# Two attention and feed-forward layer pairs on one core: fixed queue order at the start, two tiles transposed by DMA, and rstd of one chunk on ScalarE

## The chip, the cores and the metric

The kernel runs on one core of a Trainium2 chip. The metric is device time in microseconds for one whole execution, lower is better. The engines are TensorE (PE in the profile; its weight loads are PEld), VectorE (DVE), ScalarE (ACT), GpSimd (POOL) and SyncE (SP), which here only issues DMAs. Each engine works through its own queue in order; engines wait for one another by semaphores.

## The reference

Two times over, a linear attention block and a feed-forward block are added to x (2048 tokens, D = 512):

```python
x = x + A(layernorm(x));  x = x + B(layernorm(x))      # twice, with the same weights

def A(x):                         # 32 heads of 16
    q, k, v = split(x @ wqkv)
    phi = lambda t: where(t > 0, t + 1, exp(t)) + 1e-6
    kv  = einsum("bhsd,bhse->bhde", phi(k), v);  z = sum_s phi(k)
    o   = (phi(q) @ kv) / (phi(q) . z + 1e-6)
    return o @ wo                 # 512 x 512

def B(x):
    return relu(x @ w1) @ w2      # 512 -> 1376 -> 512
```

Inputs, weights and the output are bfloat16; matrix products accumulate in float32 and x is kept in float32 between the layers.

## The kernel before, in words

The tokens are cut in 16 tiles of 128, which make 4 chunks of 4 tiles. A tile has its tokens on the partitions. All of x, all weights and all intermediate results stay in on-chip memory; only x, the weights and the result are moved from and to HBM. There are four layers, 0 to 3: attention, feed-forward, attention, feed-forward.

**Attention (layers 0 and 2).** Each normalized tile xn[i] is transposed to Tb[i]. kproj i multiplies it by the k columns of wqkv (4 matmuls of 128x512, contracted over the four parts c of D). The phi function follows: ACT writes t + 1 (line 532, "lin") and exp(t) (line 534, "exp"), DVE takes the minimum with 1 (line 536, "em") and the maximum of both (line 542, "phi"). qproj t_j does the same for a chunk t and a quarter j of the q columns; it needs all four tiles of the chunk. The G groups (g_r, g_a) multiply the xn of a chunk by phi(k) and accumulate over all chunks; a column of ones, written over the last column of xn by POOL (line 582, "onec"), gives the sums z there. From G and the v weights the kernel makes kv, masks it by heads and multiplies it by wo (Mf). wv needs its last row taken off first (line 577). The denominators (den) are turned into reciprocals rdc by Ln and Exp on ACT (lines 653, 655), spread over the partitions by DMA (line 665, "spread") and multiplied into phi(q) by DVE (line 671, "pqs"). The fin matmuls multiply that by Mf, and DVE adds the result to x (line 560, "resid") with the row sums s1 as a by-product; ACT squares the new x (line 566) for the row sums of squares s2.

**Feed-forward (layers 1 and 3).** w1 times Tb of a chunk gives eleven strips h; relu is applied by ACT or DVE (lines 743, 744). The last strip, 96 wide (hr), is made transposed and turned by a DMA transpose (line 724). ffo i multiplies the strips by w2 (11 matmuls), and DVE adds x (line 560, or 557 in the last layer). In the last layer tile 15 is made in two halves of 256 columns (b_out_halves, line 748), each with its own add (line 762) and store (line 765).

**Normalization.** In the first layer the statistics come from bn_stats and bn_aggr on DVE (lines 446, 447). Tiles 0, 1 and 2 are taken one at a time (line 793): veps on DVE (811), rstd by a power on POOL (801), norm on DVE (803), then a transpose on PE against the identity (line 514) and a copy out of PSUM by ACT or DVE (518, 519, "trev"). Tile 3 has its sums from ACT (814, 816) and its variance from POOL (818 to 822, "nm2_3", "var_3", "veps_3"). Chunk 1 (tiles 4 to 7) is taken in pairs, with rstd by Ln and Exp on ACT (454, 456), norm on DVE (480) and transposes on PE. Chunks 2 and 3 are taken whole and transposed by DMA from SP (line 497, tr2_0, tr2_1, tr3_0). Between the layers, ln_next makes mean, variance, rstd and nbias of a chunk in seven small POOL instructions (462 to 474, the sixth a power of 1.0 to 1.3 us), then norms on DVE, ACT and, for the last tile of the chunk, POOL (484 to 489), and transposes by DMA. Chunk 0 of a feed-forward layer is "urgent": its transposes go in two halves.

**What sets the order.** The program builds a graph of operations with their data dependencies, and `_list_schedule` (line 136) plays it through with fixed estimates of duration. On each engine it takes the operation that can start first, and among those that could start at once the one with the lowest priority number; that number is the place in the program plus an entry of HINTS, if there is one. Operations with alternatives (add_flex) go to the engine that would finish them first. The result is a fixed queue for each engine, so the order on the chip doesn't react to real durations. Eleven matmuls on zeros warm PE up first (line 423). The loads are issued by SP in the order of the program: x of tile 0, x of tiles 1 to 3, wk, x of chunk 1, wq, x of chunks 2 and 3, wv, the last row of wv, wo, w1, w2 in two parts. The first DMA transpose also waits for wk and wq.

Of the kernel before, what the change touches and what calls it, by code (L numbers as in the profile page):

```python
# [7 lines left out]
ALU = alu_op_type.AluOpType  # L8
# [39 lines left out]
HINTS = {"0.bnag4": 3, "0.fin8_0": -99, "0.g0_1_3": 10, "0.g1_1_1": 30, "0.g1_2_1": -496, "0.g1_2_2": -77, "0.k0_em": -57,  # L48
         "0.k4_em": -180, "0.k5_em": -110, "0.pqs3_3": 37, "0.q0_0_em": 80, "0.q0_2_em": -70, "0.q0_2_phi": 30, "0.q0_3_em": 33,
         "0.q3_2_lin": 177, "0.q3_3_lin": 30, "0.resid8": -373, "0.rstd6": 20, "0.spread1_3": -17, "0.trev1": 10, "2.fin13_0":  # L50
         200, "2.fin9_0": 200, "2.g0_0_0": 80, "2.norm0": -160, "2.q3_3_lin": 3, "2.qproj3_1": 10, "2.qproj3_2": -80,
         "2.spread0_0": 3, "2.spread0_3": -230, "2.spread1_0": 30, "2.spread1_2": 57, "2.var1": 610, "3.ffo10": 84, "3.ffo15_h1":
         200, "3.ffo2": 200, "3.h1_9_0": 230, "3.h3_3_0": 83}
# [209 lines left out]
def build_kernel(nc, A_x, A_wqkv, A_wo, B_w1, B_w2, out, n_layers_pairs=2, K_STT=0, Q_STT=0, A_PE_CHUNKS=0, windows=None,  # L263
# [20 lines left out]
    with es:  # L284
# [109 lines left out]
        dma(lambda e: e.dma_start(wqkv[:, :, D:2 * D], wq_v[:, :, D:2 * D]), [], [("wk",)], 2300.0, "ld_wk")  # L394
# [15 lines left out]
        ALL_LOADS = [("wk",), ("wq",)]  # L410
# [48 lines left out]
        def ln_chunk(t):  # L459
# [8 lines left out]
            g.add(POOL, lambda e: e.tensor_tensor(var[:, sl], s2[:, sl], nm2[:, sl], ALU.add),  # L468
                  [("s2", i) for i in tl] + [("nm2", t)], [("var", i) for i in tl], C_POOL_SMALL, name="var%d" % t)
            g.add(POOL, lambda e: e.tensor_scalar(veps[:, sl], var[:, sl], INV_D, EPS, ALU.mult, ALU.max),  # L470
                  [("var", i) for i in tl], [("veps", t)], C_POOL_SMALL + 50.0, name="veps%d" % t)
            g.add(POOL, lambda e: e.tensor_tensor(rstd[:, sl], veps[:, sl], nhalf[:, 0:4], ALU.pow),  # L472
                  [("veps", t), ("nhalf",)], [("rstd", i) for i in tl], C_POOL_POW, name="rstd%d" % t)
            g.add(POOL, lambda e: e.tensor_tensor(nbias[:, sl], mean[:, sl], rstd[:, sl], ALU.mult),  # L474
                  [("mean", i) for i in tl] + [("rstd", i) for i in tl], [("nbias", t)], C_POOL_SMALL, name="nbias%d" % t)

        def ln_norm(i, first, urgent=False):
# [7 lines left out]
            if i % 4 == 3:  # L485
                g.add(POOL, ts[1], [("xres", i), ("rstd", i), ("mean", i)], [("xn", i)], ts[2], name="norm%d" % i)
                return
# [4 lines left out]
        def transpose_chunk(t, extra_reads=(), parts=1):  # L492
            n = 4 // parts
            for k in range(parts):
# [7 lines left out]
        def transpose_pe(i):  # L502
# [19 lines left out]
            if i == 0:  # L522
                part(0, 2, ("T0a",), "0a")
                part(2, 2, ("T", 0), "0b")
                return
# [43 lines left out]
        def a_k(i):  # L569
            b = alloc_bank()  # L570
            mm_group(lambda: [(psv[:, b, :], Tb[:, i, c, :], wqkv[:, c, D:2 * D], c == 0, c == 3, False) for c in range(4)],
                     [("T", i), ("wk",)] + ([("T0a",)] if i == 0 else []), [("ps", b)], 4 * C_MM512, "kproj%d" % i)
            phi_evac(b, pk_tile(i), ("big", pk_unit(i)), "k%d" % i, stt=(i % 4) < K_STT)
# [64 lines left out]
        def a_q(t, js=(0, 1, 2, 3)):  # L638
            for j in js:
# [3 lines left out]
                         [("T", i) for i in range(4 * t, 4 * t + 4)] + ([("T0a",)] if t == 0 else []) + [("wq",)], [("ps", b)], 4 * C_MM512, "qproj%d_%d" % (t, j))  # L643
# [104 lines left out]
        def b_out_halves(i):  # L748
            t, il = i // 4, i % 4
            for hf in range(2):  # L750
                b = alloc_bank()

                def mk(b=b, hf=hf):
                    mms = []
                    for c in range(NFC):
                        K = 128 if c < NFC - 1 else FLAST
                        u = h_unit(c, t)
                        mms.append((psv[:, b, 0:256], big[0:K, u * 512 + 128 * il:u * 512 + 128 * il + 128],
                                    w2[0:K, c, 256 * hf:256 * hf + 256], c == 0, c == NFC - 1, False))
                    return mms  # L760
                mm_group(mk, [("big", h_unit(c, t)) for c in range(NFC)] + W2KEYS, [("ps", b)], NFC * 110.0, "ffo%d_h%d" % (i, hf))
                g.add(DVE, lambda e, b=b, hf=hf: e.tensor_tensor(xin[:, i, 256 * hf:256 * hf + 256], psv[:, b, 0:256],  # L762
                                                                 xres[:, i, 256 * hf:256 * hf + 256], ALU.add),
                      [("ps", b), ("xres", i)], [("xinh", i, hf)], 360.0, name="resid_out%d_%d" % (i, hf))
                dma(lambda e, hf=hf: e.dma_start(tok_view(out, t, il, il + 1)[:, 0, 256 * hf:256 * hf + 256], xin[:, i, 256 * hf:256 * hf + 256]),
                    [("xinh", i, hf), ("xin", i)] + [("T", k) for k in range(NT)], [("out", "h", i, hf)], 250.0, "sth%d_%d" % (i, hf))

        def b_out(i, last_layer):
            if last_layer and LAST_HALVES and i == NT - 1:
                b_out_halves(i)  # L770
# [36 lines left out]
        def ln_first(t):  # L807
# [24 lines left out]
            for i in range(4 * t, 4 * t + 4):  # L832
                ln_norm(i, True)
                if t < FIRST_PE_CHUNKS:
                    transpose_pe(i)
            if t >= FIRST_PE_CHUNKS:
                tr_dma(t, 2 if t == 2 else 1)
# [3 lines left out]
        def tr_dma(t, parts=1):  # L841
            extra = list(ALL_LOADS) if tr_state["first"] else []
            tr_state["first"] = False
            transpose_chunk(t, extra, parts)
# [241 lines left out]
```

## Time and profile before

| | us |
|---|---|
| median of three runs | 283.12 |
| the three runs | 283.12, 282.18, 283.13 |
| the profiled execution | 282.23 |
| its span, first to last instruction | 280.5 |
| PE busy (matmuls) | 275.2 |
| ACT busy | 173.1 |
| DVE busy | 141.4 |
| POOL busy | 45.3 |

The granted TensorE clock is 1.000 over the whole span. In the views that follow, times are in microseconds from the start of the span, an "L" with a number is a line of the kernel, `out<-in` names what an instruction writes and reads, and a bracket at the end of a row gives the idle time of the engine before it and what ended it. In the chain that ended last, each row is a start, a length, and the work that held up the end in that stretch. Matmuls overlap in the records: one of 512 columns has 0.38 us of its own, while a dense stream starts one each 0.216 us. So a row of n matmuls is longer than n times the spacing.

### The profile page before, as it was taken

Reading aid. Unit: us, or ns where it says so; the run is one execution under the profiler, and the core shown is the slowest. Engines: PE = TensorE matmul, PEld = TensorE weight load, DVE = VectorE, ACT = ScalarE, POOL = GpSimd, SP = SyncE. Lnnn points to the kernel's source line nnn. Section 1 sums busy time; section 2 is a strip of 40 time slices with the busy share of each in tenths; the row PEclk is TensorE's granted clock in tenths of the full one; section 3 lists DMA queues with packets and bytes.
Section 4 is the critical chain, followed back from the end, with each engine's and each line's share of the span. In section 5 each row is a group of like instructions: output and inputs, shape, how many; then the busy total and the mean of one; then the engine's idle time right before and its main releaser. Section 6 shows DMA issues by size and latency. Waiting matters only on the chain.

```text
span 280.5 us, 4209 instructions
## 1 busy us (share of the span) xinstructions
PE 275.2 (98%) x1574; PEld 140.7 (50%) x1574; DVE 141.4 (50%) x380; ACT 173.1 (62%) x364; POOL 45.3 (16%) x122
## 2 busy tenths in 40 slices
PE   7999999999999999999999999999999999999996
PEld 2455556545554544544444455664554544454444
DVE  5999973899300361443363666279955200210222
ACT  4998988777764582677373898765884566025000
POOL 6100000055400160400040400004236100000000
PEclk9999999999999999999999999999999999999999
DMA  7999300833810054060003030084313600341012
GB/s 231 339 384 147 72 2 11 201 89 76 159 30 0 2 95 76 0 96 0 0 7 70 0 74 0 4 196 106 75 34 63 130 1 2 94 113 20 0 75 75
DMA packets 44260, 22.09 MB, mean 79 GB/s; under 512 B 34416, under 2 KB 42704, under 8 KB 44240
## 3 DMA queue, kind: packets, MB, share of 16 engines
q1 hardware_dynamic: 44240, 21.83, 32.7%
q8 instruction: 12, 0.20, 0.3%
q14 instruction: 8, 0.07, 0.1%
HBM read 7.14 MB, written 2.10 MB: 33 GB/s over the span
## 4 chain that ended last, share of the span: by engine, by line
PE 94%; DVE 2%; DMA 1%; POOL 1%; ACT 0%; issue 0%; SPq 0%; DVEq 0%; POOLq 0%
PE ps L549 93%; DMA xin<-in_A_x_dram 1%; DVE xres L560 1%; DVE bst L446 0%; POOL rstd L472 0%; DVE xn L484 0%; PE ps L514 0%; DVE big L671 0%; ACT big L532 0%; ACT Tb L518 0%; DVE xin L762 0%; SPq L389 0%; POOL mean L462 0%; DVE xn L803 0%; POOL veps L470 0%
## 5 line engine op out<-in xcount | busy, mean ns | idle before, releaser
L549 PE MATMUL ps<-w,big 128*128 128x512 bf16 (+2 forms) x363 | 77.4, 373 | 0.0
L549 PE MATMUL ps<-Tb,w 128*128 128x512 bf16 (+1 forms) x352 | 70.9, 360 | 0.0
L743 ACT ACTIVATE big<-ps 128x512 bf16<-128x512 f32 x70 | 41.8, 597 | 24.6 <-PE ps L549 24.4
L549 PEld LDWEIGHTS ps<-w,big 128*128 128x128 bf16 (+1 forms) x363 | 35.4, 98 | 40.7 <-ACT big L743 0.3
L549 PEld LDWEIGHTS ps<-Tb,w 128*128 128x128 bf16 x352 | 33.9, 98 | 32.8
L566 ACT ACTIVATE sqscr<-xres 128x512 bf16<-128x512 f32 x48 | 29.9, 623 | 31.2 <-DVE xres L560 30.9
L532 ACT ACTIVATE big<-ps 128x512 bf16<-128x512 f32 x64 | 40.8, 641 | 7.1 <-PE ps L549 6.9
L560 DVE SCALAR_TENSOR_TENSOR xres<-ps,xres 128x512 f32<-128x512 f32 x32 | 21.2, 687 | 41.2 <-PE ps L549 41.2
L534 ACT ACTIVATE escr<-ps 128x512 bf16<-128x512 f32 x64 | 41.1, 649 | 1.3 <-PE ps L549 1.3
L557 DVE TENSOR_TENSOR xin<-ps,xres 128x512 bf16<-128x512 f32 x15 | 10.4, 691 | 49.7 <-PE ps L549 49.7
L549 PE MATMUL ps<-big,xn 128*128 128x256 bf16 (+1 forms) x224 | 31.0, 288 | 0.0
L549 PE MATMUL ps<-wqkv,Tb 128*128 128x512 bf16 x128 | 29.8, 379 | 0.9 <-DVE Tb L519 0.8
L549 PE MATMUL ps<-Tb,wqkv 128*128 128x512 bf16 x128 | 30.2, 379 | 0.0
L549 PE MATMUL ps<-Mf,big 128*128 128x512 bf16 x128 | 29.1, 379 | 0.4 <-DVE big L671 0.4
L536 DVE TENSOR_SCALAR escr<-escr 128x512 bf16<-128x512 bf16 x64 | 18.1, 290 | 19.9 <-ACT escr L534 19.5
L542 DVE TENSOR_TENSOR big<-big,escr 128x512 bf16<-128x512 bf16 x64 | 26.4, 421 | 1.4
L549 PEld LDWEIGHTS ps<-big,xn 128*128 128x128 bf16 x224 | 21.5, 98 | 9.0 <-issue 0.8
L462 POOL TENSOR_SCALAR mean<-s 128x4 f32<-128x4 f32 x12 | 3.0, 246 | 122.3 <-DVE xres L560 122.3
L549 PEld LDWEIGHTS ps<-wqkv,Tb 128*128 128x128 bf16 x128 | 12.3, 98 | 15.2 <-DVE Tb L519 1.0
L549 PEld LDWEIGHTS ps<-Mf,big 128*128 128x128 bf16 x128 | 12.1, 98 | 15.5 <-DVE big L671 1.4
L549 PEld LDWEIGHTS ps<-Tb,wqkv 128*128 128x128 bf16 x128 | 12.4, 98 | 12.9
L484 DVE TENSOR_SCALAR xn<-xres,mean,rstd 128x512 bf16<-128x512 f32 x21 | 15.2, 757 | 5.6 <-POOL nbias L474 5.5
(78 smaller groups left out, 190.8 us busy)
## 6 DMA issues: line engine op xcount, KB each, us to landing
big<-rdc SPq DMA_DIRECT2D x32, 128.0 KB, 2.7
wqkv<-in_A_wqkv_dram SPq DMA_DIRECT2D x3, 512.0 KB, 7.0
xin<-in_A_x_dram SPq DMA_DIRECT2D x3, 512.0 KB, 7.8
w<-in_B_w_dram SPq DMA_DIRECT2D x1, 1376.0 KB, 13.1
w<-in_B_w_dram SPq DMA_DIRECT2D x1, 1280.0 KB, 15.2
out_dram<-xin SPq DMA_DIRECT2D x2, 512.0 KB, 2.8
wo<-in_A_wo_dram SPq DMA_DIRECT2D x1, 512.0 KB, 10.1
xin<-in_A_x_dram SPq DMA_DIRECT2D x1, 384.0 KB, 3.0
```

The source lines that it names most:

```text
L462: g.add(POOL, lambda e: e.tensor_scalar(mean[:, sl], s1[:, sl], -INV_D, None, ALU.mult), [("s1", i) for i in tl], [("mean", i) for i in tl ...
L484: ts = (POOL, lambda e: e.tensor_scalar(xn[:, i, :], src, mean[:, i:i + 1], rstd[:, i:i + 1], ALU.add, ALU.mult), C_POOL_NORM)
L532: g.add(ACT, lambda e: e.activation(dst_ap, psv[:, b, :], ACTF.Identity, bias=1.0 + 1e-6, scale=1.0), [("ps", b)], [dst_key], C_ACT_PSUM, ...
L534: g.add(ACT, lambda e: e.activation(escr[:, s, :], psv[:, b, :], ACTF.Exp), [("ps", b)], [("escr", s)], C_ACT_EXP, name=name + "_exp")
L536: g.add(DVE, lambda e: e.tensor_scalar(escr[:, s, :], escr[:, s, :], 1.0, 1e-6, ALU.min, ALU.add), [("escr", s)], [("escr", s)], C_DVE_BF4 ...
L542: g.add(DVE, lambda e: e.tensor_tensor(dst_ap, dst_ap, escr[:, s, :], ALU.max), [dst_key, ("escr", s)], [dst_key], 340.0, name=name + "_phi")
L549: last = e.matmul(o, l, r, start=st, stop=sp, skip_group_check=skip)
L557: g.add(DVE, lambda e: e.tensor_tensor(xin[:, i, :], psv[:, b, :], src, ALU.add), [("ps", b), skey], [("xin", i)], C_DVE_PSUM, name="resid ...
L560: g.add(DVE, lambda e: e.scalar_tensor_tensor(xres[:, i, :], psv[:, b, :], 0.0, src, ALU.add, ALU.add, accum_out=s1[:, i:i + 1]), [("ps", ...
L566: g.add(ACT, lambda e: e.activation(sqscr[:, q, :], xres[:, i, :], ACTF.Square, accum_out=s2[:, i:i + 1]), [("xres", i)], [("sqscr", q), ( ...
L743: g.add_flex([(ACT, lambda e, M=M, b=b, u=u: e.activation(unit_ap(u, M), psv[0:M, b, :], ACTF.Relu), C_ACT_PSUM), (DVE, lambda e, M=M, b=b ...
```

## The change

1. HINTS is replaced by a longer table (some entries stay), and SEQS is new: for each engine a list of operations of the first layer that must stand in that order. They become order dependencies before the planner runs, and operations with alternatives are fixed to the engine of the list.
2. The load of wk is split in two, by the parts c = 0, 1 and c = 2, 3. kproj0 is split alike: its first two matmuls need only the first half of Tb[0] and of wk.
3. Of chunk 1, only tiles 4 and 5 are transposed on PE. Tiles 6 and 7 are transposed by one DMA (tr1_1). By the list for SP it is issued after the last load of x, and wv, its last row and wo are issued behind it, w1 and w2 behind the last transpose of the first layer (tr3_0).
4. In ln_next for the urgent chunk, var, veps and nbias go from POOL to DVE, and the power on POOL becomes Ln and Exp on ACT; the norm of the chunk's last tile goes from POOL to DVE or ACT.
5. The last tile of the last layer is cut in 384 and 128 columns, not 256 and 256.

```diff
-HINTS = {"0.bnag4": 3, "0.fin8_0": -99, "0.g0_1_3": 10, "0.g1_1_1": 30, "0.g1_2_1": -496, "0.g1_2_2": -77, "0.k0_em": -57,
...
+HINTS = {"0.bnst6": -77, "0.bnst7": -49, "0.fin15_0": -10, "0.fin6_0": 10, "0.fin8_0": -99, "0.g0_0_3": -80, "0.g1_1_1": 93,
...
+SEQS = {
+    "dve": ["bnst0", "bnag0", "veps_0", "bnst1", "bnag1", "norm0", "veps_1", "bnst2", "trev0b", "bnag2", "veps_2", "norm1", "norm3",
+            "norm2", "trev2"],
+    "act": ["mean_3", "sq_3", "trev0a", "lnv_3", "rstd_3", "trev1", "trev3", "k0_lin", "k0_exp"],
+    "pool": ["rstd_0", "nm2_3", "var_3", "veps_3", "rstd_1", "rstd_2"],
+    "sp": ["ld_x3_0", "tr1_1", "ld_wv", "ld_wvl", "ld_wo", "tr2_0", "tr2_1", "tr3_0", "ld_w1", "ld_w2a", "ld_w2b"],
+    "pe": ["trp0a", "trp0b", "kproj0a", "trp1", "kproj0b", "trp3", "kproj1", "trp2", "kproj3", "qproj0_0", "kproj2"],
+}
...
-        dma(lambda e: e.dma_start(wqkv[:, :, D:2 * D], wq_v[:, :, D:2 * D]), [], [("wk",)], 2300.0, "ld_wk")
+        for k in range(2):
+            dma(lambda e, k=k: e.dma_start(wqkv[:, 2 * k:2 * k + 2, D:2 * D], wq_v[:, 2 * k:2 * k + 2, D:2 * D]),
+                [], [("wk", k)], 1150.0, "ld_wk%d" % k)
...
-        def ln_chunk(t):
+        def ln_chunk(t, urgent=False):
...
+            ve = DVE if urgent else POOL
+            small = C_DVE_SMALL if urgent else C_POOL_SMALL
+            g.add(ve, lambda e: e.tensor_tensor(var[:, sl], s2[:, sl], nm2[:, sl], ALU.add),
+                  [("s2", i) for i in tl] + [("nm2", t)], [("var", i) for i in tl], small, name="var%d" % t)
+            g.add(ve, lambda e: e.tensor_scalar(veps[:, sl], var[:, sl], INV_D, EPS, ALU.mult, ALU.max),
+                  [("var", i) for i in tl], [("veps", t)], small + 30.0, name="veps%d" % t)
+            if urgent:
+                g.add(ACT, lambda e: e.activation(var[:, sl], veps[:, sl], ACTF.Ln), [("veps", t)], [("var", i) for i in tl],
+                      C_ACT_TINY, name="lnv%d" % t)
+                g.add(ACT, lambda e: e.activation(rstd[:, sl], var[:, sl], ACTF.Exp, scale=-0.5), [("var", i) for i in tl],
+                      [("rstd", i) for i in tl], C_ACT_TINY, name="rstd%d" % t)
+            else:
+                g.add(POOL, lambda e: e.tensor_tensor(rstd[:, sl], veps[:, sl], nhalf[:, 0:4], ALU.pow),
+                      [("veps", t), ("nhalf",)], [("rstd", i) for i in tl], C_POOL_POW, name="rstd%d" % t)
+            g.add(ve, lambda e: e.tensor_tensor(nbias[:, sl], mean[:, sl], rstd[:, sl], ALU.mult),
+                  [("mean", i) for i in tl] + [("rstd", i) for i in tl], [("nbias", t)], small, name="nbias%d" % t)
...
-            if i % 4 == 3:
+            if i % 4 == 3 and not urgent:
                 g.add(POOL, ts[1], [("xres", i), ("rstd", i), ("mean", i)], [("xn", i)], ts[2], name="norm%d" % i)
                 return
...
+            for c0, n, key, tag in ((0, 2, "T0a", "a"), (2, 2, "T", "b")) if i == 0 and g.layer == 0 else ((0, 4, "T", ""),):
+                mm_group(lambda c0=c0, n=n: [(psv[:, b, :], Tb[:, i, c, :], wqkv[:, c, D:2 * D], c == 0, c == 3, False)
+                                             for c in range(c0, c0 + n)],
+                         [(key, i)] + [("wk", k) for k in range(c0 // 2, (c0 + n) // 2)], [("ps", b)], n * C_MM512, "kproj%d%s" % (i, tag))
...
-            for hf in range(2):
+            for f0, f1 in ((0, 384), (384, 512)):
...
             for i in range(4 * t, 4 * t + 4):
                 ln_norm(i, True)
-                if t < FIRST_PE_CHUNKS:
+                if t == 1 and i < 6:
                     transpose_pe(i)
-            if t >= FIRST_PE_CHUNKS:
-                tr_dma(t, 2 if t == 2 else 1)
+            tr_dma(t, 1 if t == 3 else 2, 1 if t == 1 else 0)
...
+        for e, names in SEQS.items():
+            seq = [byname["0." + n] for n in names]
+            for o in seq:
+                if o.alts:
+                    o.alts = [a for a in o.alts if a[0] == e]
+                    o.eng, o.emit, o.dur = o.alts[0]
+            for a, b in zip(seq, seq[1:]):
+                b.odeps.append(a)
+                b.prio = max(b.prio, a.prio + 0.01)
```

The last argument of tr_dma is how many of the parts to skip, so chunk 1 issues only its second half.

## The prediction

> **What bounds the kernel now.** I read the page first: the engine shares, then the share each engine has in the chain that ended last.
>
> ```profile
> PE 275.2 (98%) x1574; PEld 140.7 (50%) x1574; DVE 141.4 (50%) x380; ACT 173.1 (62%) x364; POOL 45.3 (16%) x122
> ...
> PE 94%; DVE 2%; DMA 1%; POOL 1%; ACT 0%; issue 0%; SPq 0%; DVEq 0%; POOLq 0%
> ```
>
> PE is the bound, but a busy PE need not run at its peak, so I looked next at the same chain in order of time.
>
> ```profile
> 8.85 4.49 PE ps L549 x20
> 13.34 0.45 PE ps L514 x8
> 13.78 2.59 PE ps L549 x12
> 16.37 0.45 PE ps L514 x8
> 16.82 173.38 PE ps L549 x1014
> ...
> 194.55 1.33 POOL rstd L472
> ...
> 197.18 0.67 DVE big L671 x2
> 197.85 0.05 issue
> 197.90 79.89 PE ps L549 x447
> ```
>
> From 8.85 us on PE is never short of work for long: 12 matmuls take 2.59 us, 0.216 us each, and 8 transposes 0.45 us. So there are only four places to gain or lose: the start before 8.85, the 16 transposes at 13.34 and 16.37, the detour over POOL and DVE before 197.90, and the tail. The timeline of PE shows the start: gaps of 0.8 us before 6.63 and some 0.65 us in the 12 transposes (12 x 0.056 = 0.67, but 7.50 to 8.85 is 1.35).
>
> ```profile
> 5.43 0.40 PE L514 MATMUL ps<-ident,xn 128*128 128x128 bf16 x4
> 6.63 1.04 PE L549 MATMUL ps<-wqkv,Tb 128*128 128x512 bf16 x4 [0.80 <-DVE Tb L519]
> 7.50 1.28 PE L514 MATMUL ps<-ident,xn 128*128 128x128 bf16 x12
> 8.85 2.76 PE L549 MATMUL ps<-wqkv,Tb 128*128 128x512 bf16 x12
> ```
>
> The timeline around 196 shows the detour: DVE's norm waits for POOL's nbias, takes 0.99 us, and the products of line 671, for which PE waits, stand behind it.
>
> ```profile
> 189.57 7.94 PE L549 MATMUL ps<-Mf,big 128*128 128x512 bf16 x36
> ...
> 196.13 0.77 POOL L484 TENSOR_SCALAR xn<-xres,mean,rstd 128x512 bf16<-128x512 f32 x1
> ...
> 196.19 0.99 DVE L484 TENSOR_SCALAR xn<-xres,mean,rstd 128x512 bf16<-128x512 f32 x1 [0.26 <-POOL nbias L474]
> 197.10 0.74 DVE L671 TENSOR_TENSOR big<-big 128x512 bf16<-128x512 bf16 x2
> ...
> 197.90 3.63 PE L549 MATMUL ps<-Mf,big 128*128 128x512 bf16 x16 [0.38 <-DVE big L671]
> ```
>
> 36 matmuls from 189.57 would end at 197.36; the next one starts at 197.90, so this stall is 0.54 us. By the same count 56 from 55.42 should end at 67.54 and the next group starts at 67.69: 0.15 us. These are all the stalls of the attention tails that the change can remove.
>
> **The change part by part.**
>
> *Transposes of tiles 6 and 7.* Eight PE transposes go: 0.45 us from the path, nothing beside it, since PE is the path. One ACT copy (0.60) and one DVE copy (0.42) go too, off the path. The row is the spacing in the stream. The Trainium skill (TensorE: Matmul & The Clock Gate, Part 4: PE-mode transpose) gives about 275 ns for one in a kernel's context, by which eight would free an estimated 2.2 us; the rows above, 0.45 us for eight, speak against that here.
>
> In their place SP issues one DMA transpose. Its landing takes 3.1 us in a quiet queue (63 us) and up to 5.9 us behind weight loads (20 us):
>
> ```profile
> DMA to landing us min/median/max: 3.1/3.1/3.2
> ```
>
> ```profile
> DMA to landing us min/median/max: 4.2/5.8/5.9
> ```
>
> Norms 6 and 7 now end at 15.92. If they stay there, T6 and T7 land at 19.1 at the best, against 17.3 now. PE has kproj5 until 17.07 and then the first G group (16 matmuls, 2.17 us), if the phi products of tiles 0 to 3 are ready; now the last of them ends at 18.7. So without other moves a hole of 0 to 1.7 us opens, and 2.6 us if the landing takes 5.9. For it speaks that DVE is full from 8 to 27 us; against it, that between 12.98 and 15.2 DVE runs three bn_stats of chunk 2 and ACT delays rstd6 from 13.2 to 14.31 before norm6, so norms 6 and 7 can move some 2 us forward once hints favour bnst6 and bnst7. The weights that would be in the queue now come later, so 3.1 is the nearer row. I take +0.2, ends 0 and +2.6.
>
> *What stands behind it on SP.* While this transpose waits for norm 7, wv, wvl and wo (issues 0.86, 0.90, 0.44) wait behind it; tr2_0 comes after them. wv is first read at 31.74 (line 577), wo near 48. At 7.0 to 10.1 us from issue to landing they are there by some 28 and 30: hidden. tr2_0 stood behind the feed-forward weights before (5.8 us) and stands behind 1.15 MB now instead of 2.7: no later than before. w1, w2a, w2b (issues 2.52, 1.16, 6.59) go behind tr3_0, whose issue ends at 28.4; with their 13.1 to 15.2 us they land by 46. First use of w1 is 67.69 and the spreads start at 47.16, so 20 us cover them; without the cover PE would wait one for one. The split of wk adds one issue (0.43) ahead of x1, wq, x2 and x3; the DMA engines are already busy then (7, 9, 9, 9 tenths in the page's first four slices of 7 us), so landing moves little: 0. POOL's ones for chunk 1 now wait for the DMA; their reader is the G group at 24.87, 5 us later: 0.
>
> *Fixed order of the first tiles.* DVE: bn_aggr of tile 1 goes before norm0, which starts at 5.2, not 4.98. PE transposes at 5.65; ACT's half copy starts 0.33 later and takes 0.38, so the first half of kproj0 starts at 6.42, not 6.63, and ends at 6.85. POOL: var_3 and veps_3 go before rstd_1. Line 816's sum is out at 5.64, then 0.19 and 0.2 to 0.4, so rstd_1 (0.56) starts at 6.2 to 6.4, not 5.74, and norm1 at 6.9, not 6.49. Transpose 1 at 7.3, its copy on ACT 0.44 later and 0.60 long, kproj1 at 8.4. From there kproj1, transpose 2, kproj3, kproj2 are 12 x 0.216 + 0.22 = 2.82, ending at 11.2; now the same work ends at 11.45. I take -0.2. Ends: -0.6 if norm1 keeps its 6.49 (kproj1 at 8.0), +0.3 if POOL's ops are as slow as its 0.40 row beside a DVE norm.
>
> *rstd of chunk 0 in ln_next.* Off POOL go var, veps, pow and nbias: 193.94 to 196.15, 2.2 us. On come two DVE smalls (0.16 each, line 452), Ln and Exp on ACT (0.2 each, lines 454, 456; ACT idles 2.67 us there) and nbias on DVE, about 1.1 us with the hand-overs: the norms start some 1.1 us earlier. POOL's norm3 moves to DVE or ACT. DVE's load: three smalls +0.5, one norm +0.53, but the other falls from 0.99 to the 0.53 that the group of line 484 has as its minimum, -0.46. Net +0.57 against 0.26 of idle time and 1.1 us of earlier start. The last spread is issued at 193.92 and lands 2.7 later, 196.6; its product (0.42) is done at 197.0, before PE wants it at 197.36. So the stalls of 0.54 and 0.15 go: -0.69 at the best; nearest to that, as the order on DVE is the planner's again, I take -0.55. The other end is +0.5: var and nbias waiting at the head of DVE's queue hold up the residuals and products behind them. What is late next is the spread itself.
>
> *Tail.* The last tile is cut 384 and 128 wide, not 256 and 256: PE has the same columns. The last add takes 0.69 us for 512 and 0.43 for 256, so about 0.30 for 128: -0.13. The last store halves; 128 KB took 1.7 and 64 KB 1.6: -0.05. Together -0.2, ends -0.3 and +0.1. The Trainium skill (DMA: Bandwidth & Descriptors, Specifications) wants at least 512 B per transfer and has read-modify-writes below it; rows become 256 B, so by it the store would not shorten, an estimated -0.1 for the tail. No row here has such a store.
>
> *Other hints* reorder work where PE has no gap: 0, and only to lose; they are in the range.
>
> **Sum.** -0.45 - 0.2 + 0.2 - 0.55 - 0.2 = -1.2 us. The profiled execution took 282.23 (span 280.5 and 1.7 around it), so 281.0 for such a one. It is 0.9 below the median 283.12; of three runs two are near 283.1 and one near 282.2 with nothing changed. From the median: 281.9. About 0.5%, 1.4 us, is what a measurement of this kernel can tell from no change.
>
> **Rivals.**
> - *All terms at their good ends:* -0.45, -0.5, 0, -0.69, -0.2 = -1.8, 281.3. The start decides: norm1 before 6.6. For it: all these waits are seen in the profile. Against: var_3 and veps_3 ahead of rstd_1. Chance 0.28.
> - *A transpose costs PE its whole duration:* if the 0.219 us that the rows of line 514 give to one counted and not the spacing, eight would free 1.75 and not 0.45: 280.6. Eight of them between two matmul groups in 0.45 us speak against it: chance 0.02. The Trainium skill's price above (same page and section) is of this kind; by it the rival would give an estimated 280.1.
> - *The rstd change does nothing and the start gives nothing:* PE still waits for the products, the start for norm1. -0.45 - 0.2 + 0.2: 282.7. Chance 0.17, within 0.5%.
> - *T6 and T7 late (slower):* PE stands at kproj6 or the projection of q for chunk 1. With norms at 15.92 and landing 5.9 later the hole is 2.6 us, which cancels the rest and adds 1.4: it decides from a landing at 21.8 on. If the products of tiles 0 to 3 slip as well, 1 to 2 us more: 284.5 to 286. For it: DVE is full, and tiles 8 and on queue behind. Against: the queue is quiet by then. Chance 0.18.
> - *Forecast:* -0.6 to -1.4, 0.35; own range 281.5 to 282.5.
>
> Faster 0.28 + 0.02 = 0.30, same 0.35 + 0.17 = 0.52, slower 0.18. Range 280.6 to 284.4: below it all good ends in an execution like the profiled one, above it the worse half of the late-T6 case.
>
> **What would show it.** Line 514 with 24 matmuls, not 32. Dense PE from about 8.5, with kproj0 in two pairs and no wait over 0.3 us until 30. A DMA transpose issued before 16 and landing 3 to 4 us later; POOL's line 472 with 10, not 12. No wait of PE for line 671. Wrong it is if PE waits for a Tb that DMA wrote, for w1, or at the head of DVE for a small op.

## The result, and the profile after

The changed kernel takes 283.43 us, the median of 11 runs (282.89 to 284.10); the kernel before, beside it on the same chip, takes 282.57 us (11 runs, 282.18 to 283.24). The ratio is 1.0030, with a 95% interval of 1.0018 to 1.0042. So it is 0.3% slower, where 1.2 us faster was forecast: a small difference, but clear of the interval and the other way. The profiled execution took 283.4 us with a span of 281.7; that of before had a span of 280.5.

The page of the changed kernel, its engine shares and the shares of each engine in the chain that ended last:

```profile
PE 275.5 (98%) x1566; PEld 140.1 (50%) x1566; DVE 138.8 (49%) x384; ACT 175.2 (62%) x370; POOL 40.3 (14%) x112
...
PE 89%; DMA 6%; DVE 3%; SPq 1%; issue 0%
```

PE has eight instructions fewer, as the edit says, and still ends later. The second line is the one to look at: PE's share of the chain fell from 94 to 89, and DMA's rose from 1 to 6. A transfer has come to stand in the path. The chain in order of time (start, duration, what) says where:

```profile
2.69 6.45 DMA xin<-in_A_x_dram
...
9.16 1.29 DVE bst L461 x2
...
14.73 0.64 DVE xn L503 x2
...
15.41 3.20 DMA Tb<-xn
...
18.65 211.48 PE ps L572 x1232
...
230.87 2.43 DMA out_dram<-xin
...
233.31 5.94 DMA Tb<-xn
...
239.30 39.81 PE ps L572 x207
```

There are two such places behind the start (the chain of before begins with a load of x too). At 15.41 it is the new DMA transpose of tiles 6 and 7. At 233.31 it is a transpose that the diff does not touch, of chunk 3 in the last layer, behind a store. PE's own waits confirm it (total us, times, longest):

```profile
PE ps L572 <- DMA Tb<-xn: 1.7, 2, 1.0
...
PE ps L572 <- DVE Tb L542: 0.3, 1, 0.3
```

That view counts from the modelled end of the matmul before. To get a ledger I counted starts of matmuls instead, with 0.216 us for each of 512 columns, as in the prediction. After against before, on PE's stream:

| place | what | us |
|---|---|---|
| 10.4 | projection of q waits for a copy of transposed tile 2 on DVE, behind two bn_stats | +0.45 |
| 13 to 17 | eight PE transposes gone | -0.45 |
| 17.5 | kproj6 waits for T6 and T7 by DMA | +1.12 |
| 64.0 | stall before one of the products of line 671 (now 696), layer 0 | -0.16 |
| 197.4 | the same stall in layer 2 | -0.54 |
| 238.2 | last strip hr of chunk 3, last layer, waits for its T by DMA | +0.90 |
| | sum | +1.32 |

PE's stream ends at 277.78 before and at 279.10 after: the same 1.32. Behind it the tail is 0.1 shorter, which gives the 1.2 us between the two spans. The medians differ by 0.86 only: the profiled execution of before, 282.23, lay 0.34 under its median, that of the changed kernel, 283.4, at its own. The eight transposes and the two stalls went away as forecast, nearly to the hundredth; the gain at the start did not come, and three waits that were not in the forecast, or in it too small, came instead.

### The profile page after: what moved, and what is told of

Same layout as the page of the kernel before. It is cut to its first block, busy times and chain, and to the rows that moved or that the text cites. A ratio compares the mean times of both kernels' runs of the same rounds, so it can differ in the third digit from the quotient of the medians.

```text
span 281.7 us, 4195 instructions
## 1 busy us (share of the span) xinstructions
PE 275.5 (98%) x1566; PEld 140.1 (50%) x1566; DVE 138.8 (49%) x384; ACT 175.2 (62%) x370; POOL 40.3 (14%) x112
## 4 chain that ended last, share of the span: by engine, by line
PE 89%; DMA 6%; DVE 3%; SPq 1%; issue 0%
PE ps L572 89%; DMA Tb<-xn 3%; DMA xin<-in_A_x_dram 2%; DVE bst L461 1%; DMA out_dram<-xin 1%; DVE xn L503 0%; SPq L408 0%; SPq L402 0%; DVE xin L580 0%; DVE Tb L542 0%; DVE mv L462 0%; DVE escr L559 0%; DVE big L565 0%; DVE xin L788 0%; DVE veps L467 0%
## 5 line engine op out<-in xcount | busy, mean ns | idle before, releaser
L572 PE MATMUL ps<-w,big 128*128 128x512 bf16 (+3 forms) x363 | 77.1, 373 | 0.0
L768 ACT ACTIVATE big<-ps 128x512 bf16<-128x512 f32 x74 | 43.9, 596 | 35.1 <-PE ps L572 34.9
L555 ACT ACTIVATE big<-ps 128x512 bf16<-128x512 f32 x64 | 40.7, 651 | 6.0 <-PE ps L572 5.9
L580 DVE TENSOR_TENSOR xin<-ps,xres 128x512 bf16<-128x512 f32 x15 | 10.4, 692 | 53.7 <-PE ps L572 53.7
L507 DVE TENSOR_SCALAR xn<-xres,mean,rstd 128x512 bf16<-128x512 f32 x25 | 15.9, 676 | 7.4 <-POOL nbias L497 7.4
```

What stands on the lines that cost most here:

```text
L507: ts = (POOL, lambda e: e.tensor_scalar(xn[:, i, :], src, mean[:, i:i + 1], rstd[:, i:i + 1], ALU.add, ALU.mult), C_POOL_NORM)
L555: g.add(ACT, lambda e: e.activation(dst_ap, psv[:, b, :], ACTF.Identity, bias=1.0 + 1e-6, scale=1.0), [("ps", b)], [dst_key], C_ACT_PSUM, ...
L572: last = e.matmul(o, l, r, start=st, stop=sp, skip_group_check=skip)
L580: g.add(DVE, lambda e: e.tensor_tensor(xin[:, i, :], psv[:, b, :], src, ALU.add), [("ps", b), skey], [("xin", i)], C_DVE_PSUM, name="resid ...
L768: g.add_flex([(ACT, lambda e, M=M, b=b, u=u: e.activation(unit_ap(u, M), psv[0:M, b, :], ACTF.Relu), C_ACT_PSUM), (DVE, lambda e, M=M, b=b ...
```

## The experiments

The theory to begin with was this ledger: the two waits for DMA make the kernel slower, and the start gives back what the transposes won. The rivals were that the work around rstd costs something that the ledger hides, and that the split of wk, which the forecast had put at nothing, is behind the losses at the start. The ratios are against runs of the kernel before beside it on the same chip (medians of it 282.43 to 282.57). They are worked out from all the runs and are not the quotients of the medians; the experiments ran on more than one chip, so between two of them the ratios say more than the medians.

| kernel | median us | ratio to before (95%) | span |
|---|---|---|---|
| changed kernel | 283.43 | 1.0030 (1.0018 to 1.0042) | 281.7 |
| tiles 6 and 7 on PE again | 282.86 | 1.0008 (1.0000 to 1.0017) | 280.9 |
| store free of Tb | 282.37 | 0.9994 (0.9984 to 1.0003) | 280.9 |
| both | 281.52 | 0.9968 (0.9956 to 0.9980) | 279.8 |
| rstd part alone, on the kernel before | 283.26 | 1.0028 (1.0017 to 1.0039) | 281.5 |
| wk in one load | 283.27 | 1.0030 (1.0017 to 1.0042) | 280.9 |
| both, wk in one load | 281.44 | 0.9966 (0.9954 to 0.9978) | 279.8 |
| store free, wk in one load | 282.08 | 0.9989 (0.9980 to 0.9997) | 280.4 |
| both, without the rstd part | 283.56 | 1.0040 (1.0027 to 1.0053) | 281.7 |
| instruction packets moved | 283.19 | 1.0036 (1.0021 to 1.0052) | 281.0 |
| both, wk whole, one product earlier | 281.28 | 0.9963 (0.9951 to 0.9975) | 279.5 |

**Tiles 6 and 7 on PE again.** The changed kernel with the eight PE transposes put back:

```diff
-    "sp": ["ld_x3_0", "tr1_1", "ld_wv", ...],
+    "sp": ["ld_x3_0", "ld_wv", ...],
...
-                if t == 1 and i < 6:
+                if t == 1:
                     transpose_pe(i)
-            tr_dma(t, 1 if t == 3 else 2, 1 if t == 1 else 0)
+            if t >= 2:
+                tr_dma(t, 1 if t == 3 else 2)
```

> The changed kernel with tiles 6 and 7 transposed on PE again and no tr1_1; everything else stays, PE's order too, but for the 8 transposes. Theory (the loss is two waits of PE for a Tb that a DMA writes, 1.12 us at 17.5 and 0.90 us at 238.2): the first wait goes, 8 transposes cost 0.45, so 0.67 us less than the changed kernel: 282.8 against 283.43 and 282.57 of the kernel before. Rival (the start's own order and a later clock are the loss, and another wait takes the place of the one removed): the same 283.4, with a wait of PE for a product or a copy of DVE between 17 and 22 us.

Measured: 282.86. PE's waits for DMA in this kernel:

```profile
PE ps L572 <- DMA Tb<-xn: 0.6, 1, 0.6
```

One of the two waits is left, that of the last layer (0.79 us by starts). The wait at 17.5 is gone; behind it another of 0.40 showed up at 22.6, where the G group wants a product of phi that DVE makes: a wait of the kind that the rival named. So the transposes by DMA win 0.45 us and lose 1.12, and without that loss 0.40 of the time is lost to the next wait in the row. The median fell by 0.57 where the theory has 0.67, but that it came so near is in part luck. Against the new wait stands a start that is 0.31 earlier, since x of chunk 1 landed at 8.83 and not at 9.13 and the wait at 10.4 fell from 0.46 to 0.19. That the wait at 17.5 is the transpose's holds; that nothing else would move does not.

**The store free of Tb.** In the graph, store_chunk names all tiles of Tb as read, although it moves xin. So a transpose that writes Tb waits until a store issued ahead of it has landed. The experiment drops that:

```diff
-  [("xin", i) for i in range(4 * t + lo, 4 * t + hi)] + [("T", i) for i in range(NT)], [("out", t, lo)],
+  [("xin", i) for i in range(4 * t + lo, 4 * t + hi)], [("out", t, lo)],
```

> The changed kernel without the rule that the stores of whole chunks and the transposes of Tb keep out of each other's way, so that the last transpose of layer 2 to 3 is issued before the stores; PE's order is the same. Theory: the wait of 0.90 us at 238.2 goes and nothing else moves: 282.5, 0.9 less than the changed kernel. Rival (PE would have waited there for something else, a relu of the strip or a bank): 283.4.

Measured: 282.37. The order of PE's instructions is the same as in the changed kernel. The waits for DMA:

```profile
PE ps L572 <- DMA Tb<-xn: 1.0, 1, 1.0
```

Here the wait at 17.4 is the one left, and the wait of the last layer is gone. One dependency that no data stand behind cost the changed kernel 1.06 us of its median (283.43 to 282.37). What else that wait needs is the subject of the experiment on instruction packets below.

**Both.** The two edits together.

> Both edits together. Theory: 0.67 + 0.90 = 1.57 us less than the changed kernel, 281.9, so 0.7 us (0.25%) faster than the kernel before. Rival: 283.0 to 283.4, since the start's 0.45 us and what else there is remain.

Measured: 281.52, 0.32% under the kernel before (0.20 to 0.44). PE's waits begin so, with no row for DMA:

```profile
PE ps L438 <- DVE wrm L431: 1.2, 1, 1.2
PE ps L572 <- ACT Tb L541: 0.4, 1, 0.4
PE ps L537 <- DVE xn L828: 0.3, 1, 0.3
PE ps L572 <- DVE big L565: 0.2, 1, 0.2
```

The first three are at the start, before 8 us; the last is the product at 22.3 again, 0.40 by starts. With the two late transposes out of the way the rest of the change is a gain: 283.43 - 281.52 is 1.91 us, against 1.12 + 0.90 in the ledger, less the 0.45 that the PE transposes take again, less 0.40 for the product, plus 0.6 at the start (the wait of 0.45 at 10.4 is gone here, and the point where the first projections and the first quarter of q are done is at 12.16, not 12.77). That adds up to 1.77. The 0.6 at the start belongs to neither edit as far as is shown: x of chunk 1 landed at 8.53 in this execution, with wk still in two loads. It is also why the kernel came out 0.4 under the 281.9 of the theory.

**The rstd part alone.** The kernel before, and of the change only `urgent` in ln_chunk and ln_norm: var, veps and nbias of chunk 0 on DVE, Ln and Exp on ACT.

```diff
+            ve = DVE if urgent else POOL
-            g.add(POOL, lambda e: e.tensor_tensor(var[:, sl], s2[:, sl], nm2[:, sl], ALU.add), ...
+            g.add(ve, lambda e: e.tensor_tensor(var[:, sl], s2[:, sl], nm2[:, sl], ALU.add), ...
...
-            if i % 4 == 3:
+            if i % 4 == 3 and not urgent:
```

> The kernel before with only the part on var, veps, rstd, nbias and the fourth norm of the urgent chunk. Theory: the stalls of 0.54 us at 197 and 0.15 us at 64 go, 281.9 against 282.57. Rival (PE then waits for the spread, or the new DVE ops hold up the residuals): 282.4 to 282.8.

Measured: 283.26, 0.28% slower than before where 0.2% faster was expected. The stall at 197 is gone as it should be, though not by an earlier norm: the norms of DVE start at 198.25, 3.89 us after the mean, and the product that PE wants stands before them, at 197.92. But in layer 0 a wait of 1.38 us has come, and its timeline (start, duration, engine) shows from what:

```profile
59.14 0.34 POOL L462 TENSOR_SCALAR mean<-s 128x4 f32<-128x4 f32 x1 [27.81 <-DVE xres L568]
...
60.24 0.16 DVE L470 TENSOR_TENSOR var<-s,nm 128x4 f32<-128x4 f32 x1
...
62.66 0.16 DVE L472 TENSOR_SCALAR veps<-var 128x4 f32<-128x4 f32 x1
...
64.28 0.16 DVE L482 TENSOR_TENSOR nbias<-mean,rstd 128x4 f32<-128x4 f32 x1
...
65.86 5.39 SPq L505 DMA_TRANSPOSE Tb<-xn  x3
```

Three instructions of 0.16 us on DVE, and 2.4 us between the first and the second, 1.6 between the second and the third: residuals and products stand in between in DVE's queue. The norms start 5.8 us after the mean, where it is 3.5 us in the kernel before (58.88 to 62.39), the transpose is issued 2.4 us later (65.86 for 63.41), and PE waits for T. So the part does not shorten the chain; it puts it in a queue.

**wk in one load.** In the changed kernel x of chunk 1 lands at 9.13, and 8.33 in the kernel before; the wait of PE at 10.4 hangs on it through DVE. This experiment undoes the split:

```diff
-        for k in range(2):
-            dma(lambda e, k=k: e.dma_start(wqkv[:, 2 * k:2 * k + 2, D:2 * D], wq_v[:, 2 * k:2 * k + 2, D:2 * D]),
-                [], [("wk", k)], 1150.0, "ld_wk%d" % k)
+        dma(lambda e: e.dma_start(wqkv[:, :, D:2 * D], wq_v[:, :, D:2 * D]),
+            [], [("wk", 0), ("wk", 1)], 2300.0, "ld_wk")
```

> The changed kernel with wk loaded by one DMA again; every queue but SP's stands as before, and kproj0a waits for the copy of T0a anyway. Theory (the split makes the load behind it, x of chunk 1, land at 8.5 to 9.2 us where it landed at 8.3, and DVE's bn_stats of tile 4, which wait for it, hold up the copy for the first projection of q and the statistics of tiles 6 and 7): x lands by 8.4, the wait of 0.45 us at 10.4 goes, T6 and T7 land some 0.7 us earlier, at 17.9, and PE is there 0.45 earlier, so that wait falls to 0.8: in all 0.8 less than the changed kernel, 282.6. Rival (x lands late because fewer loads are queued behind it, not because of the split): 283.4.

Measured: 283.27, which is no different from the changed kernel. In the profiled execution (282.61 us) everything is as the theory has it: x lands at 8.33, the wait at 10.4 is gone, T6 and T7 land 0.8 earlier, and the wait for them falls from 1.12 to 0.94 by starts (0.96 to 0.78 by modelled ends, as the view counts):

```profile
PE ps L572 <- DMA Tb<-xn: 1.5, 2, 0.8
```

But the other five runs lie between 283.10 and 283.57. The mechanism is seen in one execution and its worth in time is not settled by this kernel. The two that follow put it beside the others.

**Both, and wk in one load.**

> Tiles 6 and 7 on PE, stores free of the transposes, and wk in one DMA. Theory: x of chunk 1 is earlier but nothing waits for it there, since that version has no wait at 10.4 us: 281.5, the same as without the third edit; 281.2 if the wait for a product at 22.6 (0.4 us) goes with it. Rival: 281.9, if the first half of kproj0 now waits for the whole of wk.

Measured: 281.44, where without this edit it was 281.52: nothing. There the wait at 10.4 was gone anyway.

**Store free, wk in one load.**

> Tiles 6 and 7 by DMA as in the changed kernel, stores free of the transposes, wk in one DMA. Theory: 0.9 + 0.8 less than the changed kernel: 281.7. Rival (split without effect): 282.4, as with the stores alone.

Measured: 282.08, 0.29 under the kernel with the store free alone (0.14 by the ratios), and between the two expectations. The wait for T6 and T7 is 0.96, and there is a new one of 0.52 at 25.1 for tr2_0: issued at 19.63 behind wv, wvl and wo, landed at 25.67.

```profile
PE ps L572 <- DMA Tb<-xn: 1.2, 2, 0.8
```

Over the three pairs the split of wk costs 0.16, 0.08 and 0.29 us by the medians, and 0.00, 0.06 and 0.14 by the ratios, each less than the runs spread. Nor is the late landing the work of the split alone. In the six traced executions with wk whole, x of chunk 1 landed between 8.30 and 8.54; in the six with the split, between 8.36 and 9.23. The 8.36 is in the kernel with the instruction packets moved, below, whose loads are those of the changed kernel in the same order, and there the wait at 10.4 is gone too. So with the split the landing can be late and need not be. What decides it the traces don't show; the rival's reason, fewer loads behind it, does not suffice either, since that kernel has no more of them.

**Both, without the rstd part.** After the surprise of the rstd part alone it stood open what it is worth inside the change.

```diff
-                if i % 4 == 3 and not urgent:
+                if i % 4 == 3:
...
-            ln_chunk(t, urgent)
+            ln_chunk(t, False)
```

> Tiles 6 and 7 on PE and stores free, and the urgent chunk's var, veps, rstd, nbias and fourth norm on POOL again. Theory (that part removed the stalls of 0.54 and 0.15 us): 282.2, with a wait of PE for line 696 near 197 us. Rival (the new order of the products on DVE, which the hints give, removed them): 281.5, without such a wait.

Measured: 283.56, 2.0 us over the kernel that has it. The waits:

```profile
PE ps L572 <- DMA Tb<-xn: 1.1, 2, 0.7
...
PE ps L572 <- DVE big L696: 0.3, 1, 0.3
```

The second is the stall before the products, back at 198.6 with 0.45 us, as the theory had it and against the rival: the product stands on DVE at 198.76 again, behind a norm of 197.84. The time did not come out by the theory, which had 282.2. The two waits for DMA are at 75.0 and 105.7 (0.55 and 0.90), for transposes that the edit does not touch. The order of PE's work differs from that of the kernel compared with, since the planner laid it out around another chain, and it reads two chunks before they have landed. So of the 2.0 us the part is worth 0.45 directly; the other 1.45 come with the new order, which the same hints give around a different chain.

**Instruction packets moved.** The transpose of 233.31 took 5.94 us to land; four tiles take 4.2 to 4.3 where nothing else is under way. Where one took 5.8 to 6.0 (at 73.74 and 119.90 in the kernel before, at 210.16 and 233.31 in the changed one), one packet of 16 KB on another queue, which the profile calls the instruction queue, had started 3.8 to 4.0 us after the issue (12 such packets in the span). The DMA view of 236.5 to 239.5 us of the changed kernel shows it (packets, MB, share):

```profile
q1 hardware_dynamic: 420, 0.10, 18.2%
q8 instruction: 1, 0.02, 1.9%
```

The reverse does not hold. In the kernel before, the transpose of 145.80 had a packet 3.97 us after its issue and landed in 4.63; with tiles 6 and 7 on PE, that of 145.93 had one after 3.85 and landed in 4.24. So a packet may delay a transpose, and what decides whether it does is open.

The kernel with tiles 6 and 7 on PE shows the same thing on the store. Its packet came at 232.36 and fell on the store ahead of the transpose (timeline):

```profile
230.19 0.34 SPq L814 DMA_DIRECT2D out_dram<-xin  x1
...
234.23 1.85 SPq L520 DMA_TRANSPOSE Tb<-xn  x1
```

The store landed in 4.02 us, the transpose behind it was issued late and took its usual 4.24, and PE waited 0.79. In all twelve traces this store took 4.0 to 4.2 us in the five where a packet came some 2.2 us after its issue, and 2.3 to 2.5 in the seven others.

If these packets carry PE's instructions, one comes every 128 matmuls or so (15 to 27 us between them here), and it can be moved with nothing else changed in the program: by matmuls in the warm-up. The warm-up multiplies zeros, and no result hangs on it.

```diff
-                for k in range(WARM):
+                for k in range(3):
                     last = e.matmul(psv[:, wt, :], wrm[:, 0:128], wrm[:, :], start=True, stop=True)
+                for k in range(52):
+                    last = e.matmul(psv[:, wt, 0:32], wrm[:, 0:128], wrm[:, 0:32], start=True, stop=True)
```

> The changed kernel with its 11 warm-up matmuls of 512 columns replaced by 3 of 512 and 52 of 32 columns: 44 more matmuls, so that every later point of PE's instruction stream comes 44 instructions pairs earlier in the 16 KB pieces in which it is read in, some 9.5 us at 0.216 us a matmul. Theory (a transpose by DMA that has such a packet, 0.9 us on the instruction queue, in its last part lands 1.6 us late): the packet of 237.24 moves to about 227.7, the transpose issued at 233.3 lands 4.2 after its issue at 237.5, PE's wait of 0.90 at 238.2 goes and the time falls by 0.8 to 282.6; the transpose issued at 210.2, 5.84 until now, takes 4.2 too, and the one issued at 112.6, 4.26 until now, gets the packet of 124.8 at about 115.3 and takes 5.8, for which PE does not wait. Rival (the late landing comes from the store ahead of it or from what else stands on the queue): 5.9 at 233.3 and 5.8 at 210.2 as before, 4.3 at 112.6, wait of 0.9 still there, 283.4.

Measured: all twelve packets came earlier, by 4.6 to 10.9 us, and that of 237.24 at 227.73. So they do go with the count of PE's instructions. The transpose, issued at 233.56 behind the same store, landed at 237.80: 4.24 us. The one of 210.40 landed in 4.25, where it had been 5.84. The third one foretold, at 111.51, kept its 4.26, because its packet came at 117.54, after it, and not at 115.3; it says nothing either way. PE's last strip hr runs with no wait at 238.64 (timeline):

```profile
233.56 1.76 SPq L522 DMA_TRANSPOSE Tb<-xn  x1
...
238.64 0.84 PE L574 MATMUL ps<-w,Tb 128*128 128x96 bf16 x16
```

The store is still ahead of it, so the rival is out: order and store made the transpose start with no slack, and in the changed kernel the packet made it land late. But another packet moved too, from 192.24 to 185.92, onto the spreads of layer 2, and the chain of this kernel goes through one of those:

```profile
184.11 4.09 DMA big<-rdc
188.23 0.42 DVE big L698
188.65 0.35 DVE KVT L654
189.04 3.20 PE ps L574 x16
```

The spread issued at 184.11 took 4.09 us where the page of the changed kernel has 2.7 for spreads; DVE waited for it with KVT behind, and PE 0.46 us for KVT. By starts, as in the ledger, that is 0.62. Up to there PE was 0.39 ahead of the changed kernel, 0.3 of it from the start, with x of chunk 1 at 8.36. So the profiled execution gained 0.39 and 0.90 and lost 0.62, and with its 282.73 it is 0.67 under that of the changed kernel. The median did not come to the 282.6 of the theory. It is 283.19, only 0.24 lower than the changed kernel's, and the ratio to before, 1.0036, is not lower at all: the runs go from 282.68 to 284.20. The wait is shown to be the packet's in the trace; that moving the packets makes the kernel faster is not shown. When a packet comes is not the same in every execution (235.67 in the kernel with the store free, 237.24 in the changed kernel, with the same order on PE). That this makes the spread of the runs is an argument, not a measurement: one execution of each kernel has a trace.

**One product earlier.** The last kernel takes "both, wk in one load" and asks for the product of tile 1's phi ahead of the bn_stats of tile 13 on DVE:

```diff
-        for e, names in SEQS.items():
+        for e, names in list(SEQS.items()) + [("dve", ["k1_phi", "bnst13"])]:
```

> Tiles 6 and 7 by PE, the store free, wk whole, and the products of tile 1's phi ahead of the bn_stats of tile 13 on DVE. Theory (the only wait of PE left between 12 and 270 us, 0.37 us at 22.4, is for that product): no wait there and 281.1. Rival (another product or a copy on DVE is then last): a wait of 0.2 to 0.4 at another place before 30 us and 281.4.

Measured: 281.28 (281.08 to 281.64), 0.37% under the kernel before (0.25 to 0.49), and the waits of PE are these alone:

```profile
PE ps L438 <- DVE wrm L431: 1.2, 1, 1.2
PE ps L572 <- ACT rstd L823: 0.6, 1, 0.6
```

Both are at the start. The wait at 22.4 is gone and the median is 0.16 lower than without the edit, less than the spread of the runs. It is the fastest kernel of this case.

## Why the prediction was wrong, step by step

*Transposes of tiles 6 and 7: the step failed in its size.* The gain was right: the eight are gone, and 0.45 us with them. In the fastest kernel, where the transposes of 6 and 7 are on PE, eight others start at 13.16 and the next matmul at 13.61, 0.45 again. So the trace and not the 275 ns of the Trainium skill (TensorE: Matmul & The Clock Gate, Part 4: PE-mode transpose) gives the price here. The landing was right as well: 3.20 us for the 3.1 that was taken as the nearer row. What failed was the choice of +0.2 out of 0 to +2.6; it measured +1.12 (0.94 to 1.13 in the five traces that have this transpose). It rested on norms 6 and 7 coming forward by some 2 us; they ended at 15.38, not 15.92, half a microsecond earlier. DVE could not start on chunk 1 before 9.16, since x of that chunk had just landed (the second row is the copy for which PE waits at 10.4):

```profile
9.16 1.29 DVE L461 BATCH_NORM_STATS2 bst<-xin 128x6 f32<-128x512 bf16 x2 [0.85 <-DMA xin<-in_A_x_dram]
...
10.58 0.39 DVE L542 COPY Tb<-ps 128x512 bf16<-128x512 bf16 x1
...
14.65 0.73 DVE L503 TENSOR_SCALAR xn<-xin,mv,rstd 128x512 bf16<-128x512 bf16 x2
```

And PE had nothing to put in the hole: the G group that was named as the cover stood behind kproj6 and kproj7 in its queue. By the prediction's own way of counting, the norms' end and the landing, 15.38 + 3.2 = 18.6, against the end of kproj5 at 17.53 with nothing behind it that could run, the hole is the 1.12 us that came. A cover "if the phi products are ready" in a fixed queue is a cover only if that queue has it in front.

*Other hints, "0, and only to lose": the step that failed outright, with +0.90.* In the changed kernel the last strip hr of chunk 3 in the last layer stands 11 us further forward, at 238.2 of PE's time and not 249.24. With the rstd part alone it stays at 250.21, and in every kernel built on the changed one it stands between 237 and 240, also without the rstd part, the DMA for tiles 6 and 7 or the split of wk. So none of these moved it; the new hints and lists are left, and which entry did it is not shown. Before, its transpose was issued behind the store and landed at 247.25, 2.0 us early:

```profile
242.97 1.93 SPq L497 DMA_TRANSPOSE Tb<-xn  x1
...
249.24 0.84 PE L549 MATMUL ps<-w,Tb 128*128 128x96 bf16 x16
```

After, the planner's own times have the store landed at 232.46, the transpose at 236.80 and the strip at 236.89, with no slack (0.09 us, where the same planner had 1.13 before), and the real transpose took 5.94 us instead of 4.2. The store free of Tb (no wait), and the packets moved (no wait, store as it was), each take it away alone. "In the range" was right; a price of nothing was not. The new table has entries of 90 to 374 for layer 3, and the 2.0 us of slack that they could use up are in the trace of before; they were not read off.

*Split of wk, "landing moves little: 0".* In the profiled execution x of chunk 1 landed 0.8 us later, 9.13 for 8.33, and through DVE it made the wait of 0.45 at 10.4. In the kernel with wk in one load it landed at 8.33 and that wait was gone; but one execution with the split has it at 8.36, without the wait. So the landing can move, which the prediction put at 0, and the time followed by 0.29 us at the most.

*Fixed order of the first tiles, -0.2: it came out at +0.45, with the same wait at 10.4.* The reason given, norm1 and the transposes behind rstd_1, was not what decided. The copy of tile 2 was: on DVE it stands behind the bn_stats of tiles 4 and 5, and so behind a late x. Nor was the start any earlier up to there. The first half of kproj0 was to start at 6.42 and started at 6.80: norm0 had ended at 5.54, but the first transposes stood on PE behind the warm-up, whose matmuls ran 0.43 us apart up to 5.91 in this execution; in that of before the last ones ran 0.22 apart, and the transposes started at 5.43. The kernel with the rstd part alone, whose start is that of before, has 5.90 in its execution, so the change is not the reason. In "both", with x at 8.53 and the transposes at 5.69, the same projections are done at 12.16, where it is 12.31 in the kernel before: 0.15 us earlier, which is about the step's own size.

*rstd of chunk 0, -0.55: size right, reason wrong.* The two stalls went, -0.70. But the chain is not 1.1 us shorter; from the mean to the first norms (on ACT, at 197.47) it is 3.67 us after and 3.35 before. In the changed kernel's timeline of 193 to 198:

```profile
193.80 0.34 POOL L477 TENSOR_SCALAR mean<-s 128x4 f32<-128x4 f32 x1 [28.81 <-DVE xres L583]
...
197.28 0.16 DVE L497 TENSOR_TENSOR nbias<-mean,rstd 128x4 f32<-128x4 f32 x1
197.35 0.42 DVE L696 TENSOR_TENSOR big<-big 128x512 bf16<-128x512 bf16 x1
...
197.69 1.00 DVE L507 TENSOR_SCALAR xn<-xres,mean,rstd 128x512 bf16<-128x512 f32 x2
```

nbias comes at 197.28, and the product (line 696) now stands before the norms and not behind them. It is the order on DVE that took the stall away, and the part brings that order with it: alone on the kernel before it has the product before the norms too, and without the part the product is behind a norm again. The prediction's other end for this step, var and nbias held up at the head of DVE's queue, is what the rstd part alone showed in layer 0, with 1.38 us.

*Loads of later weights hidden, wo and w1 in time: right.* No kernel with the changed loads waited for a weight. tr2_0 behind them was no wait in the changed kernel either; with the store free and wk in one load it was one, of 0.52 us.

*Tail, -0.2: half right.* -0.1. The last add took 0.29 us, as estimated. The last store, 32 KB in rows of 256 B, landed in the same 1.6 us as the one of 96 KB beside it; before, two of 64 KB had 1.6 as well:

```profile
out_dram<-xin SPq DMA_DIRECT2D x1, 96.0 KB, 1.6
out_dram<-xin SPq DMA_DIRECT2D x1, 32.0 KB, 1.6
```

So the -0.05 for the smaller store did not come. By the Trainium skill (DMA: Bandwidth & Descriptors, Specifications), which has read-modify-writes for transfers under 512 B, it was not to come; these rows agree with that in the sum, but show no penalty over the store in rows of 512 B either.

*The rivals.* The time came out by the one called late T6 and T7 in its mechanism, at less than half its price, with a second late transpose that no rival had. The prediction's own sign of being wrong, PE waiting for a Tb that DMA wrote, came twice. That case's own sum was 0.2 off: its hole of 2.6 less the 1.4 of the other terms adds 1.2, not 1.4. Each of the two late transposes alone left the kernel within 0.1% of before: that is what the first two experiments measured. Term by term, the 2.4 us between the -1.2 of the forecast and the +1.2 between the spans are 0.92 for tiles 6 and 7, 0.90 for the other hints, 0.65 for the start, 0.1 for the tail, and 0.15 the other way for rstd.

## What to carry to other kernels

Where one engine is busy 98% of the time, a transfer gains only as much as its whole way, from the data it waits for to the landing, fits under work that already stands in front in that engine's queue; write down that queue, not the work that could be there. When an order is made by a planner with fixed durations, every place where a landing and its reader touch with less slack than landings vary (here 1.7 us) is a loss, so compare the slack of all transposes before and after, the untouched ones too. And look through the dependencies that carry no data: one of them cost about as much here, 1.06 us, as the whole change was to gain, 1.2.

## What the runs showed of the hardware

Reading PE's instructions is a load on the DMA engines that can reach the transfers of data. Twelve packets of 16 KB, 0.9 to 1.5 us each, come in the span, and 44 more matmuls at the start brought all of them 4.6 to 10.9 us forward. A transpose of four tiles that has one 3.7 to 4.0 us after its issue landed in 5.8 to 6.0 us in some places and in 4.2 to 4.6 in others; without one, and with nothing beside it, it took 4.2 to 4.3. Moving the packets away brought two from 5.94 and 5.84 back to 4.24 and 4.25, and made a spread land in 4.09 where 2.7 is usual. A store of 384 KB took 4.0 to 4.2 us with a packet 2.2 us after its issue and 2.3 to 2.5 without. Two executions of the same order can have the packet 1.6 us apart.

The first matmuls of an execution start 0.43 us apart and later ones 0.22, at a granted clock of 1.000 in these records. With eleven matmuls in the warm-up the change came at 4.63 us in the execution of the kernel before, and not before 5.9 in that of the changed kernel. The first transposes stand behind the warm-up and started at 5.43 and at 5.91.
